# w_out kept in the second halves of w1 and w2, and a new list of the steps up to the first unit's outputs

## The chip, the cores and the metric

The kernel runs on one core of a Trainium2 chip. The core's engines run side by side, each in its own order: TensorE (PE, with its weight loads PEld), VectorE (DVE), ScalarE (ACT), GpSimd (POOL) and SyncE (SP, which here issues nearly all transfers). The metric is the device time of one execution in microseconds (us), and lower is better. Before the change the median of 5 runs is 592.6 us (591.66 to 593.51).

## The reference

Two blocks in a row, all in fp32 (q, k, v and beta arrive as fp32, the four moe weights as fp64). First a gated delta rule, token by token, for 4 batches of 8 heads, 768 tokens and 48 features:

```python
k_n = k / (norm(k) + 1e-6); state = 0
for t in range(768):
    y[t] = q[t] @ state
    state = state + beta[t] * outer(k_n[t], v[t] - state.T @ k_n[t])
```

Its outputs, as 3072 tokens of 384 features x, then go through a multiplicative feed-forward block:

```python
h = ((x @ w1) * (x @ w2)) @ w3        # w1, w2: 384 x 1024, w3: 1024 x 1024
out = h @ w_out                       # w_out: 1024 x 384
```

## The kernel before, in words

**Tiling.** The 768 tokens are cut into 12 chunks of 64. A chunk m of all 32 (batch, head) pairs is handled at once; two chunks make a unit u of 512 tokens for the feed-forward block. The delta rule of a chunk is solved by inverting a unit triangular matrix; the inverse is done for two chunks together, in blocks of 32, on DVE.

**w3 and w_out are folded** into one 1024 x 384 matrix w34 on the chip (line 756, `fold`), so that the block is ((x w1)*(x w2)) w34. The fold needs w3 transposed.

**The order is written out by hand.** Each kind of work is a Python generator, and every `yield` ends a step. `ORDER` is a list of names; each name runs its generator to its next yield, and the instructions of each engine stand in that order (the list is run from line 1006 on; `in_text_order` holds them to it). In this document V0.38 means the 38th entry of V0 in the list. The names, with m a chunk, j or u a unit:

- k, q, v: load a chunk's keys, queries, values. p: eight transfers each time, two times a chunk: keys, then queries, in the layout that DVE's transpose takes (`load_perm`, line 223). K, Q: transposes of the first two chunks on PE. d: those of the later chunks, on DVE.
- P0 to P35: a piece of weights (`piece`, line 695): transfer(s) into one of five buffers `raw`, two ACT instructions, two DVE instructions, one POOL instruction, which make fp32 of the bits of fp64. P0 to P7 are w_out, P8 to P23 w3 (one transfer each); P24 to P29 w1, P30 to P35 w2 (four transfers each). Of each weight, the first three pieces are columns 0 to 511, the next three columns 512 to 1023. A piece can be loaded when the piece five earlier has left its buffer.
- t0 to t15: transpose of a piece of w3. f0 to f7: a block of the fold, in two halves of eight matmul records on PE, then a copy by ACT.
- g: sums of squares of the keys of two chunks. N: their norms (15 small DVE instructions). s: the scores of a chunk (U on DVE, PT). u: U to DRAM (four transfers). V: the inverse of two chunks: V.2 loads Ub from DRAM, V.3 and V.4 copy to PSUM on ACT, then 31 steps of two DVE instructions (V0.5 to V0.35, lines 440 and 445), two ACT copies (V0.36, V0.37) and the store of Vd to DRAM (V0.38).
- e: the corner: eight transfers of the inverse out of DRAM (T), then two products on PE. n: scaled values on POOL. c: the chain of a chunk, which carries the state (line 551). y: its outputs (line 652), then ACT copies them into xT (y.2), and six transfers move rows inside xT (y.3).
- b0 to b7: the products with w1 and w2 of unit 0's first chunk; a00 to a07: those of its second chunk; a10 to a57: those of whole units (`ab`, line 772; three matmuls with w1, ACT copy, three with w2, DVE multiply). Block jc reads columns 128 jc to 128 jc + 127 of w1 and w2. T, S: sums of weights and of slabs for a Strassen product; o: that product (line 874); x: the results and their stores.

**Where w_out lies.** w1s and w2s are tiles of 128 x 3 x 1024. Until the folds are done, w_out (1024 x 384) lies in w2s and fills all of it, `wo = w2s[:]...rearrange("p (j d) -> p j d", d=DM)`. So P30 to P35 can write w2s only when the fold's matmuls that read that stretch are done. w1s is free from the start.

**Transfers.** SP's queue issues in the order of the list. The program as built gives its transfers eight semaphores in turn, so a transfer waits until the one eight before it has landed. ACT issues k0 and q0.

Of the kernel before, what the change touches and what calls it, by code (L numbers as in the profile page):

```python
# [8 lines left out]
FP32 = mybir.dt.float32  # L9
# [39 lines left out]
N1 P30 t12 t14 t15 e0 t15 d3 f7 d3 f6 e0 P30 P21 e0 e0 P24 f7 s2 s2 e1 e0 s2 P24 e0 e1 V1 p4 s2
e1 P26 s2 e1 P25 d3 c0 P21 P30 u2 s3 c0 s3 P26 N1 P31 P24 y0 s3 s3 y0 c0 s3 s3 P25 t13 N1 e1 u3  # L50
P31 c0 P26 P31 P32 c1 V1 c1 e1 P25 V1 P27 c1 V1 c1 V1 V1 t13 V1 V1 V1 V1 V1 V1 y0 V1 P25 f7 f6
f6 P30 P32 P32 v2 V1 P27 s1 P31 V1 V1 y1 b3 b1 V1 b0 P32 P28 y1 b1 V1 b1 b3 P29 P27 b2 b3 y1 V1
P27 b1 b0 P29 P29 c1 a01 b2 a03 P28 V1 a01 a00 b3 P28 P29 a02 a02 a03 P35 P28 V1 a05 b7 a00 V1
V1 V1 V1 a06 P33 V1 b5 a05 b7 b0 V1 P34 V1 b5 V1 a06 V1 V1 V1 P34 k4 V1 P35 V1 g2 a00 V1 k5 a00
b0 V1 V1 g2 a04 P34 n2 p4 n2 a07 c1 a04 b2 b4 P33 b6 b2 P35 V1 g2 g2 P34 g2 e2 a07 g2 P33 e2
P35 c2 c2 e3 d4 a03 d4 a03 a01 P33 g2 b4 d4 g2 e2 b6 e2 a07 e2 b4 d4 T a01 T b4 e2 a07 c2 s4 p5
g2 c2 T g2 N2 V2 b6 p5 b6 s4 b5 s4 c2 a06 c2 a06 a04 v3 y2 d5 b5 d5 k6 s4 e3 d5 s4 y2 a02 a05
d5 s4 b7 a04 n3 S0 a02 a05 S0 s5 S0 u4 e3 s5 n3 s5 e3 b7 T o0 c3 c3 s5 g3 s5 S0 N2 N2 x0 e3 g3
e3 o0 s5 c3 c3 u5 o0 x0 V2 S0 x0 y3 V2 y3 S0 V2 S0 V2 S0 S0 V2 V2 V2 S0 g3 o0 S0 o0 S0 x0 V2 c3
o0 v4 y3 V2 V2 V2 x0 p6 V2 x0 V2 S0 a10 a10 S0 g3 S0 x0 V2 x0 S0 o0 x0 x0 p6 a14 V2 k7 a17 a17  # L60
a14 V2 V2 V2 a15 a16 V2 a16 a15 V2 g3 V2 V2 V2 V2 V2 v5 V2 x0 a13 V2 V2 V2 a17 a12 V2 a13 g3 V2
V2 g3 a17 c3 a14 a13 d6 d6 a11 V2 e4 n4 a12 e4 e4 c4 d6 V3 e4 a14 a10 n4 g3 d6 c4 e5 a11 e4 s6
g3 a13 e4 a12 p7 a10 c4 g3 N3 s6 c4 s6 a11 y4 n5 y4 c4 e5 a12 c4 a11 a15 c5 n5 e5 p7 a16 d7 d7
d7 d7 o1 c5 v6 a16 k8 g4 g4 e5 g4 p8 a15 g4 s7 s7 S1 e5 s7 S1 e5 x1 s7 s7 S1 s7 c5 o1 s6 S1 u7
c5 o1 s6 s6 u6 S1 S1 V3 S1 y5 c5 c5 V3 V3 V3 V3 V3 o1 S1 x1 k9 S1 y5 S1 y5 o1 S1 S1 x1 x1 V3 S1
S1 V3 c6 V3 S1 S1 V3 d8 o1 x1 x1 v7 a20 n6 x1 V3 a20 o1 x1 a23 V3 V3 x1 V3 x1 n7 a27 a24 d8 a26
V3 V3 V3 V3 x1 g4 V3 a23 V3 a25 V3 a27 a27 V3 a24 V3 V3 a26 a20 V3 g4 V3 p8 V3 V3 V3 V3 p9 V3
V3 a25 d8 n6 d8 g4 a20 a22 a22 a24 V3 c6 a27 a25 a24 a21 a21 e6 e6 e6 g4 e7 N3 e6 a25 N3 g4 s8
g4 N4 s8 e6 a22 s8 a26 e6 c6 c6 N4 s8 a26 s8 y6 a22 V4 p9 N4 S2 d9 e7 s8 a21 e7 y6 u8 d9 a21 e7
c6 a23 d9 p10 e7 d9 S2 c6 S2 s9 n7 a23 s9 e7 o2 s9 c7 s9 S2 s9 k10 S2 c7 x2 o2 c7 S2 S2 o2 u9  # L70
s9 V4 c7 V4 S2 y7 V4 V4 x2 V4 g5 g5 V4 p10 d10 y7 S2 x2 S2 o2 y7 V4 o2 x2 c7 V4 V4 S2 S2 V4 o2
a35 x2 x2 k11 x2 S2 V4 x2 S2 a35 v8 V4 S2 V4 V4 S2 V4 x2 n8 o2 a37 x2 V4 v9 V4 V4 V4 x2 a34 n8
# [17 lines left out]
def kernel(  # L90
# [14 lines left out]
    P = 128  # L105
# [85 lines left out]
    TTs = padded("TT", [P, NR, H, C], 2)  # L191
# [340 lines left out]
    xts = {}  # L532

    def scaled_v(c):
        nv = vtoks[c]
        for r in range(NR):
            pool.tensor_tensor(  # L537
                out=nv[:, r], in0=nv[:, r],
                in1=scale_of(ns, c)[:, r].unsqueeze(2).to_broadcast([P, H, D]), op=ALU.mult,
            )  # L540
            yield

    def chain(c):
        TT, nv, KQ = TTs[c % 2], vtoks[c], KQs[c]

        def products(out, lhs, rhs):
            ps = two_banks()
# [23 lines left out]
            return St[feat(h % 2), z, NP * r + h // 2, :]  # L571

        St = Ss.get(c)
        R = nv
        if c > 0:
            ps = products(
                by_tokens_of_features, lambda r, h, z: KQ[feat(h % 2), NR * z + r, h // 2, 0, :], state
            )
            yield
            R = in_turn(work, [P, NR, H, D], "R", 1, "R")  # L580
            v3, r3 = (
                x[:].rearrange("p r (a e) d -> p (r a) e d", e=2) for x in (nv, R)
            )
            dve.tensor_tensor(
                out=r3, in0=v3, in1=ps.rearrange("p e g d -> p g e d"), op=ALU.subtract
            )
            yield
# [127 lines left out]
        pool.tensor_tensor(out=du, in0=du, in1=lo, op=ALU.add)  # L715
        yield

    w1s = const.tile([P, KM, DF], FP32, name="w1s")
    w2s = const.tile([P, KM, DF], FP32, name="w2s")
    w34 = const.tile([P, KF, DM], FP32, name="w34")  # L720

    wo = w2s[:].rearrange("p m f -> p (m f)").rearrange("p (j d) -> p j d", d=DM)

    def piece_wo(j):
        return piece(DM, [(slice(0, P), moe_w_out[j * P : (j + 1) * P, :])], lambda: wo[:, j])

    def piece_w12(w, src, m, n0):
        srcs = []
        for e in range(2):
            a, b = D * (NP * e + m), D * (NP * e + NP - 1) + 16 * m  # L730
            srcs.append((slice(C * e, C * e + D), src[a : a + D, n0 : n0 + CW]))
            srcs.append((slice(C * e + D, C * e + C), src[b : b + 16, n0 : n0 + CW]))
        return piece(CW, srcs, lambda: w[:, m, n0 : n0 + CW])

    w3s, w3Ts = {}, {}

# [19 lines left out]
    def fold(jc):  # L756
        ps = bank([P, CW])
        for kc in range(KF):
            pe.matmul(  # L759
                ps[:, 0:DM], lhsT=w3Ts[jc, kc // 4][:, kc % 4 * P : kc % 4 * P + P],  # L760
                rhs=wo[:, kc], start=(kc == 0), stop=(kc == KF - 1),
            )
            if kc == KF // 2 - 1:
                yield
        yield
        act.copy(out=w34[:, jc, :], in_=ps[:, 0:DM])
        yield
# [3 lines left out]

    def ab(u, jc, c0, c1):
        x = xts[u]
        js = slice(jc * P, (jc + 1) * P)

        def product(w):
            ps = bank([P, B, c1 - c0, C])
            for m in range(KM):
                pe.matmul(  # L779
                    ps[:].rearrange("p b c t -> p b (c t)"), lhsT=w[:, m, js],  # L780
                    rhs=x[:, m, :, c0:c1].rearrange("p b c t -> p b (c t)"),
                    start=(m == 0), stop=(m == KM - 1),
                )
            return ps[:].rearrange("p b c t -> p b (c t)")
# [260 lines left out]
```

## Time and profile before

| | |
|---|---|
| median of 5 runs | 592.6 us (591.66 to 593.51) |
| the profiled execution, device time | 595.21 us |
| its span, first to last instruction | 593.5 us |
| mean granted PE clock | 0.977 |
| PE busy | 544.5 us (92%) |
| DVE, ACT, POOL busy | 361.3, 159.5, 176.5 us |
| transfers | 57.31 MB, 219508 packets |

The profile shows one execution. A busy time is a sum over the instructions of an engine; a matmul's end is modelled, so a PE that is called busy is not at its peak. A fp32 matmul counts as two records on PE. "Idle before" is time of the engine just before an instruction, with what released it. The chain that ended last is followed back from the last instruction; its shares say which work stood on that chain, and 73% of it is PE, 10% DMA, 7% DVE, 4% SP's queue. PE's busy share in 40 equal slices begins 2, 5, 6 tenths and then stands at 8 or 9 nearly everywhere, and the granted clock drops to 7 or 8 tenths in slices 7 to 10.

### The profile page before, as it was taken

To read this page: it belongs to the slowest core of one execution; us is meant where nothing else is said; L and a number is where in the kernel's file an instruction comes from. 1 tells how busy PE (TensorE), PEld (TensorE's weight loads), DVE (VectorE), ACT (ScalarE), POOL (GpSimd) and SP (SyncE) were. 2 spreads that over 40 slices of the span, in tenths; PEclk is the share of its full clock that TensorE was granted. 3 is DMA by queue.
4 is the path that set the end of the run, shared out by engine and by line. 5 is a ranking of instruction groups with operands and counts; after the bars stand their busy time and mean duration, and the time that the engine had idled before them with its cause. 6 is when DMAs were issued, how large, how long until landed. Compare 5 with 4: busy or idle time off the path is not lost.

```text
span 593.5 us, 19063 instructions
## 1 busy us (share of the span) xinstructions
PE 544.5 (92%) x8188; PEld 381.1 (64%) x8188; DVE 361.3 (61%) x828; ACT 159.5 (27%) x333; POOL 176.5 (30%) x223
## 2 busy tenths in 40 slices
PE   2569889698999999999999989999999999999997
PEld 2456546576888974558854669645697446974477
DVE  3797896678786579574796555866736924210012
ACT  4666354452512202121210222112220112311100
POOL 7563542042364601206121043111170000600051
PEclk9999997778999999999999999999999999999999
DMA  9979986776855454563553345624432040010001
GB/s 248 201 158 271 204 166 139 130 168 136 144 83 94 99 85 109 80 97 51 116 98 80 48 66 102 127 56 62 71 54 88 13 90 4 17 41 13 1 0 53
DMA packets 219508, 57.31 MB, mean 97 GB/s; under 512 B 206657, under 2 KB 212801, under 8 KB 219425
## 3 DMA queue, kind: packets, MB, share of 16 engines
q1 hardware_dynamic: 215232, 55.31, 46.3%
q10 hardware_dynamic: 4192, 0.79, 1.0%
q8 instruction: 64, 1.05, 0.8%
q14 instruction: 20, 0.16, 0.1%
HBM read 43.88 MB, written 11.01 MB: 92 GB/s over the span
## 4 chain that ended last, share of the span: by engine, by line
PE 73%; DMA 10%; DVE 7%; SPq 4%; issue 3%; ACT 2%; POOL 0%; ACTq 0%; DVEq 0%; POOLq 0%
PE ps_f L779 42%; PE ps_f L874 17%; PE ps_w L551 5%; DMA raw<-in_moe_w_dram 4%; PE ps_w L652 4%; PE ps_w L498 2%; DMA Ub<-Ud 2%; PE ps_w L367 1%; DVE tb L440 1%; DVE ps_w L445 1%; DMA ktok<-in_k_dram 1%; PE ps_w L373 1%; SPq L414 1%; DMA vtok<-in_v_dram 1%; SPq L230 1%
## 5 line engine op out<-in xcount | busy, mean ns | idle before, releaser
L779 PE MATMUL ps_f<-xT,w2s 128*128 128x512 f32 (+1 forms) x336 | 131.8, 538 | 1.8 <-issue 1.8
L779 PE MATMUL ps_f<-xT,w1s 128*128 128x512 f32 (+1 forms) x336 | 129.8, 539 | 2.2 <-ACT raw L708 2.2
L846 POOL TENSOR_TENSOR ab<-ab 128x256 f32<-128x256 f32 x96 | 67.0, 726 | 177.4 <-DVE ab L795 155.3
L779 PEld LDWEIGHTS ps_f<-xT,w1s 128*128 128x128 f32 x336 | 64.5, 194 | 58.4 <-issue 52.7
L779 PEld LDWEIGHTS ps_f<-xT,w2s 128*128 128x128 f32 x336 | 62.1, 190 | 54.7 <-issue 51.6
L791 ACT COPY ab<-ps_f 128x512 f32<-128x512 f32 (+1 forms) x56 | 28.2, 526 | 170.3 <-PE ps_f L779 166.1
L874 PE MATMUL ps_f<-w,ab 128*128 128x192 f32 x376 | 66.5, 330 | 0.0
L795 DVE TENSOR_TENSOR ab<-ab,ps_f 128x512 f32<-128x512 f32 (+1 forms) x56 | 33.0, 603 | 52.8 <-PE ps_f L779 52.6
L874 PEld LDWEIGHTS ps_f<-w,ab 128*128 128x128 f32 x376 | 61.1, 190 | 4.4 <-issue 3.5
L440 DVE TENSOR_TENSOR tb<-Vb,Ub 128x31 f32<-128x31 f32 (+15 forms) x124 | 43.6, 352 | 19.4 <-DMA Ub<-Ud 16.1
L874 PE MATMUL ps_f<-room,ab 128*128 128x192 f32 x272 | 47.9, 330 | 1.9 <-DVE room L905 1.9
L445 DVE TENSOR_TENSOR Vb<-Vb,tb 128x31 f32<-128x31 f32 (+15 forms) x124 | 46.5, 375 | 4.3
L759 PE MATMUL ps_f<-w2s,w3T 128*128 128x384 f32 x128 | 46.2, 517 | 0.0
L874 PEld LDWEIGHTS ps_f<-room,ab 128*128 128x128 f32 x272 | 44.1, 190 | 2.8 <-issue 2.3
L673 ACT COPY xT<-ps_w 48x256 f32<-48x256 f32 x96 | 30.5, 365 | 55.8 <-PE ps_w L652 55.2
L270 POOL TENSOR_TENSOR sq<-ktok 128x384 f32<-128x384 f32 x24 | 20.9, 875 | 69.7 <-DMA ktok<-in_k_dram 62.3
L759 PEld LDWEIGHTS ps_f<-w2s,w3T 128*128 128x128 f32 x128 | 25.4, 204 | 16.8 <-issue 2.8
L537 POOL TENSOR_TENSOR vtok<-vtok,n 128x384 f32<-128x384 f32 x24 | 20.0, 845 | 43.2 <-DMA vtok<-in_v_dram 43.2
L367 PE MATMUL ps_w<-KQ 48*64 48x128 f32 x384 | 29.5, 293 | 1.7 <-DVE PT L397 1.7
L373 PE MATMUL ps_w<-KQ 48*64 48x64 f32 x768 | 29.9, 232 | 0.0
L715 POOL TENSOR_TENSOR w<-w,raw 128x512 uint32<-128x512 uint32 x16 | 20.9, 1310 | 27.7 <-ACT raw L708 4.4
L373 PEld LDWEIGHTS ps_w<-KQ 48*64 48x64 f32 x768 | 27.1, 146 | 0.1
(109 smaller groups left out, 659.0 us busy)
## 6 DMA issues: line engine op xcount, KB each, us to landing
raw<-in_moe_w_dram SPq DMA_DIRECT2D x16, 512.0 KB, 6.3
vtok<-in_v_dram SPq DMA_DIRECT2D x24, 192.0 KB, 4.3
raw<-in_moe_w_dram SPq DMA_DIRECT2D x24, 192.0 KB, 4.4
out_dram<-osb SPq DMA_DIRECT2D x46, 96.0 KB, 2.3
ktok<-in_k_dram SPq DMA_DIRECT2D x44, 96.0 KB, 3.8
raw<-in_moe_w_out_dram SPq DMA_DIRECT2D x8, 384.0 KB, 4.0
Ud<-U SPq DMA_DIRECT2D x48, 64.0 KB, 2.5
Ub<-Ud SPq DMA_DIRECT2D x6, 512.0 KB, 4.3
```

Source lines behind the costliest of these rows:

```text
L367: pe.matmul(ps[half(z), 0, n : n + 128], lhsT=x[:, 0, :], rhs=x.rearrange("p j t -> p (j t)"), start=True, stop=True,)
L373: pe.matmul(ps[half(z ^ j), 1, n + C * j : n + C * j + C], lhsT=x[:, 0, :], rhs=x[:, j, :], start=True, stop=True,)
L440: dve.tensor_tensor(out=tv, in0=V[:, 0 : s + 1, s : s + 1].to_broadcast([P, s + 1, n]), in1=U[:, s, s + 1 : BS].unsqueeze(1).to_broadcast( ...
L445: dve.tensor_tensor(out=o, in0=o, in1=tv, op=ALU.subtract)
L551: pe.matmul(out(ps, r, h, z), lhsT=lhs(r, h, z), rhs=rhs(r, h, z), start=True, stop=True,)
L673: act.copy(out=xT[f, p:NP:2, b : b + NR, cc, :].rearrange("p a r t -> p r a t"), in_=pyv[f, z, b : b + NR],)
L759: pe.matmul(ps[:, 0:DM], lhsT=w3Ts[jc, kc // 4][:, kc % 4 * P : kc % 4 * P + P], rhs=wo[:, kc], start=(kc == 0), stop=(kc == KF - 1),)
L779: pe.matmul(ps[:].rearrange("p b c t -> p b (c t)"), lhsT=w[:, m, js], rhs=x[:, m, :, c0:c1].rearrange("p b c t -> p b (c t)"), start=(m = ...
L791: act.copy(out=t, in_=ps)
L795: dve.tensor_tensor(out=t, in0=t, in1=ps, op=ALU.mult)
L846: pool.tensor_tensor(out=o_, in0=x_, in1=y_, op=op)
L874: pe.matmul(ps[b][:, b, :], lhsT=abs_[u, HF * f + i][:, t0 : t0 + P], rhs=ws_[w][:, i], start=first and i == 0 and (b == 0 or n == "F"), s ...
```

## The change

w_out now lies in the second halves of two tiles: w1s and w2s become 128 x 2 x 3 x 512 (half of the columns first), w_out's first four blocks lie in the second half of w1s and its last four in the second half of w2s. So the pieces of columns 0 to 511 (P24 to P26, P30 to P32) can be written at any time, and those of columns 512 to 1023 (P27 to P29, P33 to P35) only when the fold's matmuls that read there are done. The products `ab` address a half and a block in it.

The list's first 725 entries are permuted: the same names, each as often. The other 592 entries, from the first unit's outputs on, are unchanged. Two stretches of the list are shown, the beginning and that from the last steps of V0 to the first products of unit 0 (old first, then new). In `chain` and `scaled_v` the lookup of the values' tile is moved into the place of use, so that v may come later in the list.

```diff
 ORDER = """
-V0 P0 k0 beta P18 P13 P0 P18 P0 P0 P18 P18 g0 P11 beta P13 K0 K0 P11 P10 q0 P10 P3 k1 P11 P13
-K0 beta P12 g0 P3 K0 g0 K0 g0 P13 K1 g0 P8 P12 g0 K1 K1 P11 P9 Q0 Q0 g0 Q0 P10 P12 g0 Q0 Q0 g0
...
-P15 t6 P20 t7 V0 n1 P22 P20 V0 t7 d2 s0 V0 V0 f3 P23 P20 P22 t8 P21 V0 n0 P24 n0 f3 V0 V0 n1 t8
-V0 V0 t9 V0 V0 s2 p3 f4 f3 P23 P22 P26 g1 V0 g1 V0 f4 g1 P21 P22 P23 t14 d3 f4 P23 g1 t12 p3 V0
-N1 P30 t12 t14 t15 e0 t15 d3 f7 d3 f6 e0 P30 P21 e0 e0 P24 f7 s2 s2 e1 e0 s2 P24 e0 e1 V1 p4 s2
-e1 P26 s2 e1 P25 d3 c0 P21 P30 u2 s3 c0 s3 P26 N1 P31 P24 y0 s3 s3 y0 c0 s3 s3 P25 t13 N1 e1 u3
-P31 c0 P26 P31 P32 c1 V1 c1 e1 P25 V1 P27 c1 V1 c1 V1 V1 t13 V1 V1 V1 V1 V1 V1 y0 V1 P25 f7 f6
-f6 P30 P32 P32 v2 V1 P27 s1 P31 V1 V1 y1 b3 b1 V1 b0 P32 P28 y1 b1 V1 b1 b3 P29 P27 b2 b3 y1 V1
-P27 b1 b0 P29 P29 c1 a01 b2 a03 P28 V1 a01 a00 b3 P28 P29 a02 a02 a03 P35 P28 V1 a05 b7 a00 V1
-V1 V1 V1 a06 P33 V1 b5 a05 b7 b0 V1 P34 V1 b5 V1 a06 V1 V1 V1 P34 k4 V1 P35 V1 g2 a00 V1 k5 a00
-b0 V1 V1 g2 a04 P34 n2 p4 n2 a07 c1 a04 b2 b4 P33 b6 b2 P35 V1 g2 g2 P34 g2 e2 a07 g2 P33 e2
-P35 c2 c2 e3 d4 a03 d4 a03 a01 P33 g2 b4 d4 g2 e2 b6 e2 a07 e2 b4 d4 T a01 T b4 e2 a07 c2 s4 p5
...
+P12 k0 P0 K0 V0 P12 P12 P11 beta P0 P12 P8 P10 P11 P0 P8 P0 P1 P9 K0 g0 P8 P10 g0 g0 K0 P11 K0
+beta K0 q0 P9 k1 K1 P10 beta g0 P11 t4 P10 g0 K1 P2 K1 K1 q1 g0 P9 K1 g0 P8 g0 Q0 g0 t4 P9 g0
...
+t11 V0 t6 t8 f5 d2 n0 P21 P22 P24 t8 t6 P20 P20 f4 d2 f5 V0 V0 t9 t9 P21 s0 n1 f3 P23 t7 V0 f4
+p3 P23 V0 t7 P22 s1 V0 V0 n0 f4 s2 g1 P20 f3 V0 g1 V0 f3 P23 t12 g1 P22 g1 t15 t12 t15 P22 p3
+V0 P26 t14 d3 t14 f6 P24 g1 V1 N1 P24 P26 e0 e0 f7 e1 e0 s2 f7 s2 e0 e0 P30 e0 d3 s2 P30 P26 e1
+P21 s2 P21 s2 P26 p4 c0 c0 P24 d3 e1 d3 y0 t13 P25 e1 s3 s3 s3 y0 P31 s3 P25 c0 s3 s3 u2 P31 u3
+P32 t13 N1 e1 V1 e1 P29 c0 n1 c1 y0 P31 c1 V1 N1 P25 c1 V1 P32 P30 c1 P32 f7 P30 f6 P32 f6 y1
+P27 P29 P25 V1 V1 V1 b0 P28 b1 V1 V1 V1 V1 b0 V1 P31 V1 V1 V1 V1 P33 b0 b0 V1 y1 V1 V1 b2 V1 b1
+b1 c1 b2 y1 P27 P28 b2 b3 a00 b1 P29 a00 P33 a03 b3 v2 b2 P27 a02 P28 P34 P28 V1 a01 a02 V1 a01
+P27 P29 a00 V1 V1 V1 a03 V1 V1 a04 b7 V1 a00 V1 P34 V1 V1 k4 k5 V1 V1 b6 b7 V1 a04 b6 a01 V1
+a01 a06 V1 P34 g2 b3 g2 V1 g2 a06 P35 b3 b4 a05 b4 d4 a07 n2 P35 P35 P33 c1 p4 a05 V1 a03 n2
+P34 b5 e2 g2 P33 P35 a02 b5 c2 e2 a02 a07 e2 g2 g2 b5 c2 e2 g2 e2 a03 a05 g2 e3 a05 e2 d4 a06
...
@@ -532,16 +532,15 @@
     xts = {}
 
     def scaled_v(c):
-        nv = vtoks[c]
         for r in range(NR):
             pool.tensor_tensor(
-                out=nv[:, r], in0=nv[:, r],
+                out=vtoks[c][:, r], in0=vtoks[c][:, r],
                 in1=scale_of(ns, c)[:, r].unsqueeze(2).to_broadcast([P, H, D]), op=ALU.mult,
             )
             yield
 
     def chain(c):
-        TT, nv, KQ = TTs[c % 2], vtoks[c], KQs[c]
+        TT, KQ = TTs[c % 2], KQs[c]
 
         def products(out, lhs, rhs):
             ps = two_banks()
@@ -571,7 +570,7 @@
             return St[feat(h % 2), z, NP * r + h // 2, :]
 
         St = Ss.get(c)
-        R = nv
+        R = vtoks.get(c)
         if c > 0:
             ps = products(
                 by_tokens_of_features, lambda r, h, z: KQ[feat(h % 2), NR * z + r, h // 2, 0, :], state
@@ -579,7 +578,7 @@
             yield
             R = in_turn(work, [P, NR, H, D], "R", 1, "R")
             v3, r3 = (
-                x[:].rearrange("p r (a e) d -> p (r a) e d", e=2) for x in (nv, R)
+                x[:].rearrange("p r (a e) d -> p (r a) e d", e=2) for x in (vtoks[c], R)
             )
             dve.tensor_tensor(
                 out=r3, in0=v3, in1=ps.rearrange("p e g d -> p g e d"), op=ALU.subtract
@@ -715,14 +714,17 @@
         pool.tensor_tensor(out=du, in0=du, in1=lo, op=ALU.add)
         yield
 
-    w1s = const.tile([P, KM, DF], FP32, name="w1s")
-    w2s = const.tile([P, KM, DF], FP32, name="w2s")
+    w1s = const.tile([P, 2, KM, CW], FP32, name="w1s")
+    w2s = const.tile([P, 2, KM, CW], FP32, name="w2s")
     w34 = const.tile([P, KF, DM], FP32, name="w34")
 
-    wo = w2s[:].rearrange("p m f -> p (m f)").rearrange("p (j d) -> p j d", d=DM)
+
+    def wo(j):
+        x = (w1s, w2s)[2 * j // KF][:, 1].rearrange("p m f -> p (m f)")
+        return x[:, j % (KF // 2) * DM : j % (KF // 2) * DM + DM]
 
     def piece_wo(j):
-        return piece(DM, [(slice(0, P), moe_w_out[j * P : (j + 1) * P, :])], lambda: wo[:, j])
+        return piece(DM, [(slice(0, P), moe_w_out[j * P : (j + 1) * P, :])], lambda: wo(j))
 
     def piece_w12(w, src, m, n0):
         srcs = []
@@ -730,7 +732,7 @@
             a, b = D * (NP * e + m), D * (NP * e + NP - 1) + 16 * m
             srcs.append((slice(C * e, C * e + D), src[a : a + D, n0 : n0 + CW]))
             srcs.append((slice(C * e + D, C * e + C), src[b : b + 16, n0 : n0 + CW]))
-        return piece(CW, srcs, lambda: w[:, m, n0 : n0 + CW])
+        return piece(CW, srcs, lambda: w[:, n0 // CW, m])
 
     w3s, w3Ts = {}, {}
 
@@ -758,7 +760,7 @@
         for kc in range(KF):
             pe.matmul(
                 ps[:, 0:DM], lhsT=w3Ts[jc, kc // 4][:, kc % 4 * P : kc % 4 * P + P],
-                rhs=wo[:, kc], start=(kc == 0), stop=(kc == KF - 1),
+                rhs=wo(kc), start=(kc == 0), stop=(kc == KF - 1),
             )
             if kc == KF // 2 - 1:
                 yield
@@ -771,13 +773,14 @@
 
     def ab(u, jc, c0, c1):
         x = xts[u]
-        js = slice(jc * P, (jc + 1) * P)
+        hf, jx = divmod(jc, KF // 2)
+        js = slice(jx * P, (jx + 1) * P)
 
         def product(w):
             ps = bank([P, B, c1 - c0, C])
             for m in range(KM):
                 pe.matmul(
-                    ps[:].rearrange("p b c t -> p b (c t)"), lhsT=w[:, m, js],
+                    ps[:].rearrange("p b c t -> p b (c t)"), lhsT=w[:, hf, m, js],
                     rhs=x[:, m, :, c0:c1].rearrange("p b c t -> p b (c t)"),
                     start=(m == 0), stop=(m == KM - 1),
                 )
```

## Prediction

> **What bounds the kernel now.** I read the stages first, by cutting the profiled execution at events of the chain that ended last. The columns are the stretch in us, busy time and instructions of PE, PEld, DVE, ACT and POOL, the granted PE clock, the DMA share and GB/s:
>
> ```profile
> 0.00:51.30 51.30, 27.88 (x509) 23.67 (x510) 33.93 (x64) 30.64 (x56) 31.31 (x43) 0.97 0.93 213
> 51.30:84.10 32.80, 30.41 (x151) 18.48 (x149) 29.26 (x80) 14.80 (x27) 15.39 (x15) 1.00 0.91 211
> 84.10:104.50 20.40, 16.70 (x284) 10.56 (x283) 15.61 (x37) 10.23 (x18) 6.26 (x6) 0.83 0.72 137
> 104.50:141.50 37.00, 28.24 (x724) 23.79 (x724) 26.43 (x62) 18.42 (x42) 9.45 (x8) 0.82 0.67 138
> 141.50:146.30 4.80, 4.76 (x13) 3.48 (x14) 4.54 (x11) 0.41 (x2) 1.98 (x2) 0.64 0.70 179
> 146.30:270.00 123.70, 122.90 (x2097) 90.29 (x2099) 90.36 (x212) 29.20 (x67) 40.63 (x52) 1.00 0.59 100
> 270.00:593.50 323.50, 313.62 (x4420) 210.79 (x4420) 161.18 (x367) 55.82 (x124) 71.48 (x100) 1.00 0.29 57
> ```
>
> From 146.3 us to the end PE is busy 436.5 of 447.2 us at clock 1.00: it is the bound there, and the new list moves no step across its unchanged last 592 entries. Before 146.3 us PE is not the bound. So the end moves by what the start of PE's dense stretch moves, corrected by PE work done ahead of it. What sets that start is read from the chain that ended last (start, us, what):
>
> ```profile
> 45.78 5.46 DMA Ub<-Ud
> ...
> 88.41 3.84 DMA Vd<-Vb
> ...
> 104.47 0.91 PE ps_w L551 x38
> ...
> 141.55 21.72 PE ps_f L779 x90
> ```
>
> First the loads and scores until the inverse V0 gets its input (Ub); then V0 on DVE, 51.3 to 84.1 us, where DVE is busy 29.26 of 32.80 us; then V0's result through DRAM and into the corner e0; then chain c0 at 104.5; then a01, the first product with both chunks of tokens, at 141.5. Between these the SP queue, which issues the transfers in order, holds the chain:
>
> ```profile
> 73.64 8.57 SPq L230 DMA_DIRECT2D kperm<-in_k_dram  x8
> 82.31 1.82 SPq L699 DMA_DIRECT2D raw<-in_moe_w_dram  x4
> 84.23 4.08 SPq L230 DMA_DIRECT2D qperm<-in_q_dram  x8
> 88.41 0.43 SPq L453 DMA_DIRECT2D Vd<-Vb  x1
> ...
> 136.13 5.28 SPq L684 DMA_DIRECT2D xT<-xT  x6
> ```
>
> ACT ends V0.37 at 85.2 us, but Vd goes out at 88.4: p3, P26 and p3 stand ahead. The last row is y1.3, whose fourth transfer has landed at 141.4; a01's first matmul reads rows of the first and the fourth. PE waits for it, and then runs slowly:
>
> ```profile
> 138.39 0.94 PE L551 MATMUL ps_w<-X,ktok 64*48 64x48 f32 x64
> 141.54 12.66 PE L779 MATMUL ps_f<-xT,w1s 128*128 128x256 f32 x48 [2.21 <-ACT raw L708]
> ```
>
> The releaser named there, ACT's conversion of P28, belongs to columns that a01 does not read, so I take the transfer.
>
> **The change, part by part.** Instructions and transfers are the same in number and size; only addresses and order differ.
>
> *Place of w_out.* Before, w_out fills all of w2s, so P30 to P32 wait for the folds. ACT shows both waits: 5.56 us ahead of P30 at 96.65 us, and
>
> ```profile
> 127.82 0.48 ACT L766 COPY w<-ps_f 128x384 f32<-128x384 f32 x1 [5.30 <-PE ps_f L759]
> 128.20 0.67 ACT L707 ACTIVATE w2s<-raw 128x512 f32<-128x512 f32 x1
> ```
>
> the second for f6 ahead of P32. After, P24 to P26 and P30 to P32 go into free halves, and P27 to P29 and P33 to P35 wait for f6.2 instead. Nothing on the chain reads P30 to P32 before b1.3 at 134.4, so the two waits are worth nothing by themselves; what they allow is ACT's order. The new wait costs nothing either: in ACT's queue P29 stands directly behind f6.3, which waits for the same matmuls, and behind P29 stand b0.2 and y1.2. P29's two instructions take 0.66 us each, and y1.2 would be done about 130 us, ahead of its transfer's turn (below). Without that cover it would cost 1.3 us.
>
> *To V0's input.* Fifteen pieces of weights, k0 to k2, q0, q1 and one p stand ahead of Ub in both lists. k1 comes one piece later (pieces land 1.3 to 2.0 us apart at 11 to 16 us) and q0 about 4 us later on ACT, but ACT's 4.06 us wait for P12 at 22.1 is gone. Step by step from the rows: k1 landed about 20.5, K1 copied out 23.1, Q0 on PE to 25.6, the sums of squares across at 26, P1.3, then norms (3.7 us) to 31, P2.3 and four U products among DVE's other steps to 37.8, eight Ud transfers (5.9 us) to 43.7, landed 1.5 later: Ub issued at 45.4 against 45.8. Bounds 41 and 52. V0 then holds 32 us of DVE work against 31, so V0.37 is done at 85 to 86, about as before.
>
> *V0's way out.* P26's four issues (1.82 us) move behind Vd. Each transfer on this queue waits for the one eight before it, by the program's own semaphores, so p3's second part now waits for its first part alone (landed 82.3 to 84.6) and not for P26 (85.4 to 87.1): Vd goes out at 86.0, 2.4 us earlier. Bounds: 3.2 if SP is quite free, 0 if p3 takes as long as before. With its 3.84 us, e0's transfers start at 89.9 against 92.3.
>
> *To the a steps.* On SP from there to y1.3 stood 43.8 us. v2 (1.4) goes behind y1.3 and two pauses (1.9 and 0.9, a wait for U and one for a transfer) can close; P30 (2.1, ahead of e0 before) and P33 (2.0) come in. With pauses closed, 43.8 - 1.4 - 2.8 + 4.1 = 43.7; part of the transfers' waits on each other falls too (P28 and P29 took 3.1 and 2.6 us, against 1.8 for a like piece at 120.8), so I take 43.0, bounds 39 and 47. y1.3 starts at 132.9, its fourth transfer lands 5.3 us later, 138.2 against 141.4: **3.2 us**. y1 itself is not late: e1.3 stands behind c0.1 now, not ahead of it (it waited for T1 until 103.3), so c0.1 is at 101.0, and y1.1 at about 122.5 against 127.7.
>
> *Work done ahead.* Seven b products instead of six stand ahead of the first a on PE. Six matmul records of 256 columns take 1.3 us in the dense stretch: **1.3 us**.
>
> *The clock.* a01 and a03 took 2.2 and 2.5 us between starts against 1.3, at a granted clock of 0.64: 2.1 us lost. b0.1 waits for y0.3's fourth transfer, about 126.1; seven b's and c1.5 end at 136.2; PE waits 2.0 us for 138.2. That is like the 2.21 us before, so I count **0** of this; bounds 0 and 2.1.
>
> The Trainium skill, page "TensorE: Matmul & The Clock Gate", Part 1, says the clock is halved after an idle window of about 3.4 us. The row is harsher: 2.21 us without a matmul, behind thin ones, already came with 0.64. By the page the new wait would cost no clock and the sum would gain 2.1 us more; I go by the row.
>
> *Behind 146 us.* The steps up to o1 are also permuted (c4 ahead of most a1 steps), PE-bound before and after with DVE at 90 of 124 us. I count 0, bounds -3 (new stalls) and +1 (PE was idle 0.8 us).
>
> Sum: 3.2 + 1.3 + 0 = 4.5 us. The profiled span 593.5 becomes 589.0; with the 1.7 us around it, 595.2 becomes 590.7. The median of the runs shown is 592.6, 2.6 below the profiled execution, so the forecast for it is **588.1 us**.
>
> **Rivals.**
>
> *Saturated sooner.* If SP reaches y1.3 by 130 (the lower bound 39 us), the a's follow the b's without a pause, and y1.1's 5.2 us count in full, with the 2.2 us wait and the 2.1 of clock: 9.5 us, 583.1. For it: y1.1 has moved more than y1.3. Against: SP's rows sum to more.
>
> *Nothing moves.* If SP keeps its pauses and waits, 47 us from e0 to y1.3, the a's start at 142.2: 0.7 us later, paid by the seventh b, 592.0. It is also the case that w_out's place does nothing and the list only permutes work around the same SP queue.
>
> *Slower: the first loads.* DMA is at 0.93 in the first 51 us, so loads land in the order of issue. k2 is issued after P7, which waits on POOL for P8: about 24 against 21.3; its squares stand on DVE ahead of three of the U products. q1 took 8.0 us to land before. If q0 or k2 takes that long again behind a fuller queue, both norms and U slip 4 to 8 us and Ub is issued at 50 to 53. V0.37 passes SP's 86.0 for each us beyond 46, and all behind it shifts. It decides from Ub at 50.3 (4.5 us eaten); at 54 the time is 596. For it: seven pieces ahead of k1, not six. Against: ACT's 4 us at P12 is free.
>
> **How the numbers follow.** Forecast with its own range 585 to 591: 0.52. Saturated sooner, under 585: 0.20. Nothing moves: 0.10. Slower: 0.18. 0.2% of 592.6 is 1.2 us, about what a measurement can tell from no change. Faster 0.72, same 0.10, slower 0.18. The range 580.5 to 595 takes in the bounds on SP and half of the slow case, and leaves out about 0.05 below and 0.10 above.
>
> **What would show it.** In the profile after: Ub issued near 45; Vd out at 86, with only p3 ahead; no ACT wait ahead of P32; the xT transfers of y1 from 133; the first a near 138 with a PE wait of about 2 us before it and a clock under 1 behind it. I am wrong if Ub is issued after 48, if PE runs from y1 into the a's without a pause, or if a wait of more than 1 us on DVE or POOL opens between 146 and 270.

## The result, and the profile after

The changed kernel takes 596.84 us (median of 54 runs, 592.2 to 601.45), the kernel before 593.96 us (median of 94 runs, 589.96 to 601.87). The ratio is 1.0038, with a 95% interval of 1.0026 to 1.0051: about 2.3 us slower. (The ratio goes with the means, 596.3 to 594.1 us without the three slowest runs, which were disturbed; the medians lie further apart.) The forecast was 588.1 us, with a range of 580.5 to 595.

The profiled execution of the changed kernel is one of its shorter ones: 594.73 us, span 593.0, clock 0.971 (before: 595.21, 593.5, 0.977). The single traces differ by several us within one kernel, so two spans compared say nothing here. What can be compared are stretches, and waits that come back in every trace of one list.

The stages of the changed kernel, cut at the same times as before (stretch, busy time of PE, PEld, DVE, ACT, POOL, granted clock, DMA share, GB/s):

```profile
84.10:104.50 20.40, 18.73 (x426) 12.79 (x429) 17.59 (x45) 8.41 (x15) 6.26 (x7) 1.00 0.64 127
104.50:141.50 37.00, 28.12 (x647) 22.98 (x637) 22.98 (x55) 19.36 (x42) 7.07 (x6) 0.72 0.77 152
...
146.30:270.00 123.70, 121.46 (x2188) 88.74 (x2187) 96.21 (x216) 29.51 (x69) 44.13 (x55) 1.00 0.61 102
```

From 84 to 104 us PE was busy 2 us more than before, but in the next stretch the clock was 0.72 and not 0.82, and from 146 to 270 us PE was busy 121.46 us and not 122.90. The chain that ended last, between the first inverse and the products (start, us, what):

```profile
87.63 3.83 DMA Vd<-Vb
...
103.47 4.37 DMA raw<-in_moe_w_dram
...
129.03 2.19 DMA xT<-xT
...
131.35 8.61 PE ps_f L782 x30
```

Vd goes out 0.8 us sooner than before (88.41), not 2.4. Then P30's transfer stands on the chain, and at the end the rows of y0.3, not those of y1.3. SP's queue, in order of time (start, us, what), shows why:

```profile
87.63 0.43 SPq L453 DMA_DIRECT2D Vd<-Vb  x1
...
125.36 5.70 SPq L683 DMA_DIRECT2D xT<-xT  x6
131.15 5.63 SPq L698 DMA_DIRECT2D raw<-in_moe_w_dram  x12
137.47 4.64 SPq L683 DMA_DIRECT2D xT<-xT  x6
```

ACT in the same order, from P30's conversion on, with the idle time ahead of an instruction in brackets:

```profile
107.95 0.66 ACT L706 ACTIVATE w2s<-raw 128x512 f32<-128x512 f32 x1 [6.71 <-DMA raw<-in_moe_w_dram]
...
109.17 1.18 ACT L514 COPY T<-ps_w 32x512 f32<-32x512 f32 x2
```

From Vd to y0.3 SP issues 58 transfers in 37.7 us; before, 54 in 34.3 us (88.41 to 122.70). That is 0.64 to 0.65 us each in both, so the four more (P26's) are 2.6 of the 3.4 us (an estimate from these rows). So y0.3 is at 125.4 and y1.3 at 137.5 (before: 122.7 and 136.1). On ACT, P30's conversion waits 6.71 us for its transfer, with e1.4 and y0.2 behind it. PE then waits for y0.3 ahead of the first b (its row):

```profile
131.35 4.63 PE L782 MATMUL ps_f<-xT,w1s 128*128 128x256 f32 x12 [1.58 <-DMA xT<-xT]
```

Later PE stops once more:

```profile
176.53 0.66 PE L651 MATMUL ps_w<-KQ,S 48*48 48x64 f32 x32
177.01 0.89 PE L550 MATMUL ps_w<-X,ktok 64*48 64x48 f32 x61
179.33 0.29 PE L550 MATMUL ps_w<-X,ktok 64*48 64x48 f32 x3 [1.43 <-issue]
179.55 4.15 PE L782 MATMUL ps_f<-xT,w2s 128*128 128x256 f32 x18
```

These rows are y2.1's end and c2.5, 64 records of one product. After 61 of them PE stands 1.43 us, and the profile names no releaser ("issue"). The old list has no stop there.

### The profile page after: what moved, and what is told of

Its sections match the earlier page's. It is cut to its first block, busy times and chain, and to the rows that moved or that the text cites. A ratio compares the mean times of both kernels' runs of the same rounds, so it can differ in the third digit from the quotient of the medians.

```text
span 593.0 us, 19060 instructions
## 1 busy us (share of the span) xinstructions
PE 543.4 (92%) x8188; PEld 379.4 (64%) x8188; DVE 365.0 (62%) x828; ACT 159.8 (27%) x333; POOL 176.6 (30%) x223
## 4 chain that ended last, share of the span: by engine, by line
PE 75%; DMA 8%; DVE 6%; SPq 4%; issue 3%; ACT 3%; ACTq 0%; POOL 0%; DVEq 0%; POOLq 0%
PE ps_f L782 43%; PE ps_f L877 17%; PE ps_w L550 5%; PE ps_w L651 3%; PE ps_w L498 2%; DMA Ub<-Ud 2%; DMA ktok<-in_k_dram 2%; PE ps_w L367 2%; SPq L230 1%; PE ps_w L373 1%; DMA raw<-in_moe_w_dram 1%; DMA X<-in_q_dram 1%; DVE tb L440 1%; SPq L462 1%; ACT KQ L347 1%
## 5 line engine op out<-in xcount | busy, mean ns | idle before, releaser
L440 DVE TENSOR_TENSOR tb<-Vb,Ub 128x31 f32<-128x31 f32 (+15 forms) x124 | 45.5, 367 | 16.8 <-DMA Ub<-Ud 13.3
L445 DVE TENSOR_TENSOR Vb<-Vb,tb 128x31 f32<-128x31 f32 (+15 forms) x124 | 45.2, 364 | 4.3
L379 DVE TENSOR_TENSOR U<-ps_w,wt 128x512 f32<-128x512 f32 x24 | 16.4, 687 | 26.9 <-PE ps_w L373 26.1
L367 PEld LDWEIGHTS ps_w<-KQ 48*64 48x64 f32 x384 | 23.3, 144 | 12.6 <-ACT T L514 4.6
L373 PEld LDWEIGHTS ps_w<-KQ 48*64 48x64 f32 x768 | 26.9, 146 | 0.0
```

What stands on the lines that cost most here:

```text
L367: pe.matmul(ps[half(z), 0, n : n + 128], lhsT=x[:, 0, :], rhs=x.rearrange("p j t -> p (j t)"), start=True, stop=True,)
L373: pe.matmul(ps[half(z ^ j), 1, n + C * j : n + C * j + C], lhsT=x[:, 0, :], rhs=x[:, j, :], start=True, stop=True,)
L440: dve.tensor_tensor(out=tv, in0=V[:, 0 : s + 1, s : s + 1].to_broadcast([P, s + 1, n]), in1=U[:, s, s + 1 : BS].unsqueeze(1).to_broadcast( ...
L445: dve.tensor_tensor(out=o, in0=o, in1=tv, op=ALU.subtract)
```

## The experiments

A ratio is to the kernel before, measured beside it on the same chip, with its 95% interval. Moves are written with entry numbers: c2.5 is the fifth c2 of the list. A line of a diff shows a few entries in their order, and other entries can stand between them. The kernels start from the changed one unless the text says otherwise.

**place_only** and **list_only** take the two parts of the change alone. The first is the changed kernel with the old list (its diff begins as below), the second the old kernel with the new list:

```diff
-P12 k0 P0 K0 V0 P12 P12 P11 beta P0
+V0 P0 k0 beta P18 P13 P0 P18 P0 P0
...
```

> The list of before, with w_out in the second halves of w1 and w2. Theory A (the new list lost the time, above all by ACT's wait for P30's transfer, 101.2 to 107.95 us in the profile after, with e1.4 and y0.2 behind it): the place alone is worth 0, 593 to 595 us, ACT's 5.3 us wait ahead of P32 is gone and P27 takes a wait for f6.2 in its stead. Theory B (the place costs: new waits of P27 to P29 and P33 to P35 for f6.2): 1 to 3 us slower than before.

> The new list, with w_out in w2 as before. Theory A: as the changed kernel within 1 us (ratio 1.002 to 1.005), since P30 waits for its transfer and not for the fold, and only P32 waits 1 to 2 us for f6.2. Theory B: as before (ratio 1.000). If the new place is what lets the new list run, 2 us slower than the changed kernel.

place_only: 592.88 us against 592.39, ratio 1.0010 (0.9986 to 1.0034). No cost or gain of the place by itself is seen. list_only: 596.95 us, 1.0069 (1.0044 to 1.0094, 6 runs), nearest to the third case forecast, 2 us slower than the changed kernel. Without the place, P32's conversion stands ahead of f6.2 in the list and writes into w_out's last blocks, so the fold reads overwritten values, and PE waits 2.6 us for P32 ahead of f6.2. So the place is what lets this list compute the right thing, and the list is where the time is. Theory B fell.

**p30_late** takes P30's conversion on ACT out of the way of e1.4 and y0.2:

```diff
-e0.6 P30.2 e1.4 y0.2 P25.2
+e0.6 e1.4 y0.2 P30.2 P25.2
```

> The changed kernel with one step moved: P30's two ACT instructions behind y0.2 and not ahead of e1.4. Theory A: e1.4 starts near 104 and not at 109.2, s3, c0.3 and c1.1 follow 3 to 5 us sooner, U is stored sooner and y1.3 with it; 2 to 4 us faster than the changed kernel, ratio to before 0.997 to 1.001. Theory C (the loss stands in the first loads: Ub landed at 53.3 and not at 51.2): the same as the changed kernel, ratio 1.004, since SP's queue to y1.3 has no room. Theory D (the loss stands behind 146 us, where DVE is busy 96 us and not 90): the same as the changed kernel too.

595.19 us, 1.0043 (1.0021 to 1.0065): nothing won, so theory A fell. ACT's rows show where the gain went:

```profile
104.59 1.18 ACT L514 COPY T<-ps_w 32x512 f32<-32x512 f32 x2 [2.91 <-PE ps_w L498]
...
108.40 0.68 ACT L706 ACTIVATE w2s<-raw 128x512 f32<-128x512 f32 x1
...
118.00 0.67 ACT L706 ACTIVATE w1s<-raw 128x512 f32<-128x512 f32 x1 [8.33 <-DMA raw<-in_moe_w_dram]
```

e1.4 is at 104.6 and not 109.2, and c1.1 starts at 113.7 and not 118.4, as forecast. But ACT then waits 8.33 us for P25's transfer with e1.6 behind it, and c1.3 is at 122.6, 1.0 us later than in the changed kernel. The wait moved to the next transfer that SP issues late.

**early_after** has the new list to V0.2 and then what is left in the old order.

```diff
-V0.2 k3.1 V0.3 d2.2 P4.3 P18.2 g1.4 f0.1 t2.2
+V0.2 P18.2 P18.3 P18.4 t2.2 s1.7 t10.1 P14.1 g1.4
...
```

> The changed kernel's list up to the load of Ub (V0.2), then what is left in the order of before; w_out in its new place. Theory C (the first loads cost the 2 us): Ub lands near 53 us, the inverse and all behind it 2 us later, ratio to before 1.003 to 1.005. Theories A and D: the early part costs nothing that lasts, ratio 0.999 to 1.001.

599.52 us, 1.0127 (1.0104 to 1.0150, 6 runs), more than any theory gave. It settles nothing: Ub goes out at 46.8 as in the new list, but what is left of the old order does not fit the pieces already loaded, DVE waits 9.0 us for ACT's conversions between 45 and 95 us, and V0.37 ends at 93.2 and not 87.1.

**thin_apart** moves one step, c2.5, behind the next big product:

```diff
-y2.1 c2.5 a04.3
+y2.1 a04.3 c2.5
```

> The changed kernel with the last products of c2 (c2.5, 64 matmul records) behind a04.3 and not directly behind y2.1 (128 records). In three traces of the new list PE stops inside c2.5, at its record 2245, for 1.4 to 1.9 us with no releaser, and the two traces of the old list have no such stop there. Theory E (some 250 short records in a row outrun what feeds PE's queue): the stop is gone or under 0.5 us, 1 to 2 us faster than the changed kernel, ratio to before 1.000 to 1.003. Theory F (the stop is a wait for c2.5's operands or banks): it stays, ratio 1.004.

593.77 us against 593.94, 1.0006 (0.9975 to 1.0037). The same place in its trace:

```profile
178.23 0.67 PE L651 MATMUL ps_w<-KQ,S 48*48 48x64 f32 x32
178.82 1.56 PE L782 MATMUL ps_f<-xT,w2s 128*128 128x256 f32 x6
180.32 0.84 PE L550 MATMUL ps_w<-X,ktok 64*48 64x48 f32 x55
181.45 0.33 PE L550 MATMUL ps_w<-X,ktok 64*48 64x48 f32 x9 [0.30 <-issue]
```

The stop is down from 1.43 to 0.30 us, and the time is that of the kernel before. That is theory E's forecast, not theory F's.

**y_first** brings the first outputs forward on ACT and SP:

```diff
-V1.2 P29.1 y0.3 P27.1 P28.1 P33.1 y1.3 v2.1
+V1.2 y0.3 P29.1 P27.1 P28.1 y1.3 P33.1 v2.1
-f6.3 y1.1 P29.2 b0.2 y1.2 b1.2 b2.2 P27.2
+f6.3 y1.1 y1.2 b0.2 b1.2 b2.2 P29.2 P27.2
-a00.2 P33.2 b3.2 a02.2        P28.4 P27.4 P29.4
+a00.2 b3.2 a02.2 P33.2        P29.4 P27.4 P28.4
```

> The changed kernel with the first outputs ahead on ACT and SP: y1.2 directly behind y1.1, P29's transfers and conversion behind y0.3 and y1.2, P33's behind y1.3. Theory G (SP's queue, at 0.65 to 0.68 us for each transfer, sets the start of PE's dense stretch; the new list has 57 transfers from Vd to y0.3 where the old one has 53): y0.3 starts near 123 and not at 125.4, b0.1 near 130 and not at 131.4, y1.3 near 135 and not at 137.5; 1.5 to 3 us faster than the changed kernel, ratio to before 0.999 to 1.002. Theory E alone (the loss is the stop in c2.5): the a's and b's start sooner but the time is that of the changed kernel within 1 us.

596.70 us, 1.0052 (1.0019 to 1.0084). All that was forecast of the places came: y0.3 at 122.3 (125.4), b0.1 at 129.9 (131.4) with no wait, the first a at 140.1 (143.5). The time did not follow. PE gives part of it back (its rows; DVE's product of a00 frees a bank late, and the clock falls behind the stop):

```profile
146.61 4.18 PE L782 MATMUL ps_f<-xT,w1s 128*128 128x256 f32 x18
152.82 2.03 PE L782 MATMUL ps_f<-xT,w2s 128*128 128x256 f32 x6 [2.03 <-DVE ab L798]
```

**y_first_thin** has y_first's edits and thin_apart's:

```diff
-y2.1 c2.5 a04.3
+y2.1 a04.3 c2.5
```

> Both edits of the two kernels before this. Theories E and G together: their gains add, 2.5 to 5 us faster than the changed kernel, ratio to before 0.996 to 1.000. If one of them is wrong: no better than the other alone.

593.94 us against 593.94, 1.0010 (0.9984 to 1.0036). The step c2.5 is worth 2.8 us in the medians; y_first's edits add nothing to it.

**k0_first** puts the first loads about as before:

```diff
-P12.1 k0.1 P0.1 K0.1 V0.1 P12.2 P12.3 P11.1 beta.1 P0.2
+k0.1 P0.1 K0.1 V0.1 beta.1 P12.1 P11.1 P0.2 P0.3 P12.2 P12.3
```

> The changed kernel with the first loads in about the order of before: P0, k0 and beta ahead of P12 and P11. Theory C (the loss comes from the first loads: k0's last part lands at 12.0 and not at 9.1 us, Ub at 53.3 and not at 51.2): k0 lands near 9, Ub 1 to 2 us sooner, and 1 to 2 us faster than the changed kernel, ratio 1.000 to 1.002. Theory G: the inverse ends 1 to 2 us sooner but Vd still goes out near 87.5 behind p3, so within 0.5 us of the changed kernel, ratio 1.003 to 1.005.

594.69 us, 1.0023 (0.9995 to 1.0051). Ub went out at 46.2 (47.5) and Vd at 86.3 (87.6), so Vd followed, against theory G's number. A gain of 1 us is possible, but the intervals of the two kernels overlap, and in k0_thin (below), with the same first loads, Ub went out at 47.7 and Vd at 89.7: not settled. In this trace the stop was 1.89 us, and the clock behind it was halved:

```profile
178.00:180.00 2.00, 0.50 (x4) 0.45 (x5) 1.54 (x8) 1.52 (x5) 0.00 (x0) 0.99 0.54 74
180.00:182.00 2.00, 2.00 (x6) 1.54 (x6) 1.96 (x3) 0.00 (x0) 0.00 (x0) 0.50 0.70 94
```

**k0_thin** is k0_first with thin_apart's move, a third pair with and without the stop:

```diff
-y2.1 c2.5 a04.3
+y2.1 a04.3 c2.5
```

> The changed kernel with k0_first's order of the first loads and thin_apart's place of c2.5: a third pair with and without the stop in c2.5. Theory E (the stop costs 1.3 to 1.9 us and now and then 1.4 to 1.8 us of clock behind it): 1.5 to 3 us faster than k0_first, ratio to before 0.997 to 1.001. If the two earlier pairs were chance: the time of k0_first, ratio 1.001 to 1.004.

592.31 us against 593.15, 0.9986 (0.9961 to 1.0011), as theory E said, and c2.5 runs without a stop:

```profile
179.47 0.94 PE L550 MATMUL ps_w<-X,ktok 64*48 64x48 f32 x64
```

It has the lowest ratio of the complete kernels, and the measurement can't tell it from the kernel before.

**thin_joined** makes the same neighbourhood in the old kernel:

```diff
-c2.5 a06.3 c2.6 a06.4 a04.3 v3.1 y2.1
+y2.1 c2.5 a06.3 c2.6 a06.4 a04.3 v3.1
```

> The kernel before with one step moved: y2.1 (128 short matmul records) directly ahead of c2.5 (64 records), as in the new list; all else, w_out's place too, is of before. Theory E (short records in a row outrun the feed of PE's instructions): a stop without releaser of 1.3 to 1.9 us inside c2.5, which ends 1.2 to 1.6 us after an instruction packet, in some runs with the clock at 0.5 for 3.4 us behind it; 1.5 to 3 us slower than before, ratio 1.002 to 1.005. Theory H (the two thin_apart kernels were faster by another effect of the moved step): no stop, ratio 0.999 to 1.001.

594.97 us against 594.12, 1.0014 (0.9990 to 1.0038): a miss of theory E. PE waits 0.5 us for DVE ahead of c2.5 and stops only 0.3 us inside it, not 1.3 to 1.9. Short records side by side are not enough; see the next section.

**u_first** and **u_first2** try to start the second inverse sooner, on top of k0_first, y_first and thin_apart:

```diff
-p4.1 P25.1 P31.1 u2.1 u3.1 P32.1 V1.2
+p4.1 u2.1 u3.1 V1.2 P25.1 P31.1 P32.1
-P30.2 e1.4 y0.2 P25.2 P31.2 t13.2 e1.6 V1.3 V1.4
+e1.4 y0.2 P30.2 t13.2 e1.6 V1.3 V1.4 P25.2 P31.2
-P31.3 c1.2 P25.3 P30.3 c1.4        V1.28 a00.4
+c1.2 c1.4 P30.3 P25.3 V1.7 P31.3   V1.24 a00.4
```

> The changed kernel with all the edits so far (k0, y and thin) and with the second inverse's way ahead: on SP the two stores of U and the load of Ub (V1.2) ahead of P25, P31 and P32; on ACT P30, P25 and P31 converted behind y0.2 and V1.4; on DVE c1.2 and c1.4 ahead of the conversions, and a00.4 earlier. Theory J (after y_first the bound from 130 to 166 us is DVE's second inverse, which ended at 157.5 whatever SP did, and it starts when SP gets to U and Ub): Ub lands near 121 and not at 127 to 129, the inverse ends near 153, c2.1 runs near 160 and not 164 to 166; 3 to 5 us faster than y_first_thin, ratio to before 0.992 to 0.997. If DVE is not the bound there: the time of y_first_thin, ratio 0.999 to 1.002. If b0.1 waits for P25 and b0.3 for P31, now later on SP: ratio above 1.000.

> As u_first, but nothing of the first outputs stands behind a transfer of P31 or P32: on ACT f7.3, f6.3 and y1.2 ahead of P31's and P32's conversions, on DVE P25's, P31's and P32's conversions inside the second inverse, on PE b0.1, b1.1, b2.1 ahead of b0.3. In u_first b0.1 waited 5.6 us for f6.3, which stood behind P32's landing on ACT. Theory J (DVE's second inverse bounds the stretch to 166 us): b0.1 near 130, the inverse ends at 153 to 155 and not 157.5 to 160.6, c2.1 near 161 to 163; 2 to 4 us faster than y_first_thin, ratio to before 0.994 to 0.998. If DVE is not the bound: the time of y_first_thin, ratio 0.999 to 1.002.

u_first: 595.96 us, 1.0019 (0.9990 to 1.0048). Ub's load was issued at 116.8 and not 122, but f6.3 now stood on ACT behind P32's landing, and b0.1 waited 5.6 us for its bank. u_first2 put these in order:

```diff
-P25.2 P31.2 P32.2 f7.3 f6.3 y1.2     b0.1 b1.1 b0.3 b2.1
+P25.2 f7.3 f6.3 y1.2 P31.2 P32.2     b0.1 b1.1 b2.1 b0.3
```

It took 598.14 us, 1.0068 (1.0030 to 1.0106). V1.5 began at 121.3 and not 127 to 129, but V1.37 still ended at 159.3. Neither kernel tells what bounds this stretch: they made waits of their own.

**half_thin** and **half_yf** are thin_apart and y_first_thin with DVE relieved: 15 of the 31 subtractions of the second inverse are left out.

```diff
-            dve.tensor_tensor(out=o, in0=o, in1=tv, op=ALU.subtract)
+            if j != 1 or s % 2 == 0:
+                dve.tensor_tensor(out=o, in0=o, in1=tv, op=ALU.subtract)
```

> thin_apart with 15 of the 31 subtractions of the second inverse (V1) left out, so the inverse of chunks 2 and 3 is not complete: about 5.5 us less DVE work between 129 and 158 us. Theory J (DVE's second inverse is where early starts of PE are given back): V1.37 ends near 152 and not at 158.5, but PE's dense stretch still starts at 132 behind y0.3, so little is won: 0 to 1.5 us faster than thin_apart, ratio to before 0.998 to 1.001. If DVE's chain alone sets the end: 4 to 5 us faster, ratio 0.992.

> y_first_thin with the same 15 subtractions left out (the inverse of chunks 2 and 3 is not complete). Theory J: the stops of PE at a01.3 and e2.3 (1.9 and 1.2 us in y_first_thin) go, and the 3 us by which the first products start sooner stay: 2 to 4 us faster than half_thin and than y_first_thin, ratio to before 0.993 to 0.997. If the gain of y_first is lost elsewhere (clock, SP, PE's feed): as half_thin, ratio 0.998 to 1.001.

half_thin: 593.75 us, 1.0014 (0.9984 to 1.0043). half_yf: 595.01 us, 1.0017 (0.9989 to 1.0045). No gain is seen, so DVE alone is not it, and theory J's gain of 2 to 4 us did not come. In half_yf V1.37 ended at 152.3, but the store of its result stayed where it was, as SP's queue shows:

```profile
153.05 5.43 SPq L230 DMA_DIRECT2D qperm<-in_q_dram  x8
158.58 0.43 SPq L454 DMA_DIRECT2D Vd<-Vb  x1
162.17 1.90 SPq L463 DMA_DIRECT2D TT<-Vd  x4
```

PE's rows, c2.1 and e2.3, have the wait that follows:

```profile
162.20 1.15 PE L551 MATMUL ps_w<-S,KQ 48*64 48x48 f32 x64
166.43 1.13 PE L499 MATMUL ps_w<-T,U 33*33 33x32 f32 x64 [3.09 <-DVE T L482]
```

**half_vd** moves that one transfer:

```diff
-p4.2 V1.38
+V1.38 p4.2
```

> half_yf (15 of the 31 subtractions of the second inverse left out) with its result's store to DRAM (V1.38) ahead of p4's eight transfers on SP. In half_yf V1.37 ended at 152.3, 5.2 us sooner than in y_first_thin, but the store went out at 158.6 as before, behind p4, and PE stopped 3.3 us for e2.3 at 166.4. Theory K (SP's queue takes back what DVE or the first products win): the store goes out near 153, e2's transfers near 158.7 and not 162.2, e2.3 follows c2.1 at 163 with no stop over 0.5 us, and the time is 2 to 4 us below half_yf's, ratio to before 0.994 to 0.999. If the stop is not SP's, or what follows takes the gain back again: ratio 1.000 to 1.003.

591.90 us against 592.75, 0.9986 (0.9957 to 1.0015): 0.0031 or 1.8 us below half_yf, with intervals that overlap. SP's queue:

```profile
153.71 0.37 SPq L454 DMA_DIRECT2D Vd<-Vb  x1
154.12 5.93 SPq L230 DMA_DIRECT2D qperm<-in_q_dram  x8
160.10 2.08 SPq L463 DMA_DIRECT2D TT<-Vd  x4
```

And PE at the same two steps:

```profile
162.77 1.15 PE L551 MATMUL ps_w<-S,KQ 48*64 48x48 f32 x64
164.35 0.75 PE L499 MATMUL ps_w<-T,U 33*33 33x32 f32 x64 [0.43 <-DVE T L482]
```

e2's transfers start at 160.1 (forecast 158.7), and PE's stop is 0.43 us and not 3.09. So with DVE relieved it is SP's turn for one store that decides here whether PE stops; the time follows by about the size of the stop, as far as the intervals allow to say. In the complete kernel y_first_thin both have to come together: there V1.37 ends at 157.5 and the store goes out at 158.6, so this move alone could win 1 us at most, and it was not tried.

## Why the prediction was wrong

**The loss is the stop in c2.5.** The step of the prediction that failed here is "Behind 146 us ... I count 0". Its bounds (-3 for new stalls) would have held the loss, but the only stalls named as signs were waits on DVE and POOL; what came is a wait of PE for its own instructions. Three pairs of kernels differ only by the place of c2.5: 1.0038 and 1.0006, 1.0052 and 1.0010, 1.0023 and 0.9986. Each pair's intervals overlap, but the three differences are 0.0032, 0.0042 and 0.0037, on average 0.0037 or 2.2 us, which is all of the 2.3 us that the change lost. (Worked out from the six intervals, the average is good to about 0.0022, so it is clear of zero.) The traces give the same size: in the five traces with the two steps joined in the new list the stop is 1.31 to 1.91 us (mean 1.6), and in two of the five the clock is 0.5 for 3.4 us behind it, which costs the next products 1.7 us (18 records in 5.84 and 5.83 us, 4.15 in the changed kernel). 1.6 + 2/5 x 1.7 = 2.3.

What PE waits for is read from the packets of the "instruction" kind that the trace records, 16384 bytes each. There are 64 of them (queue q8 of the page), and PE runs 16376 matmuls and weight loads and 168 other instructions, some 258 for each packet. Around the stops without releaser (us):

```
kernel                       PE stops          packet            PE goes on after its end by
changed, c2.5                177.91 to 179.33  176.67 to 177.94  1.39
p30_late, c2.5               179.44 to 181.34  178.88 to 179.76  1.58
list_only, c2.5              179.78 to 181.35  179.16 to 180.12  1.23
y_first, c2.5                178.70 to 180.02  177.84 to 178.80  1.22
k0_first, c2.5               177.61 to 179.50  177.15 to 178.08  1.42
before, record 5038          344.33 to 346.12  343.38 to 344.82  1.30
```

In all five c2.5 stops PE halts at the same record, 2245, and goes on 1.2 to 1.6 us after the packet's last byte. No row names a releaser, so that PE waits for the packet is inferred, but the traces leave little room for another reading.

Number all of PE's matmuls, weight loads and other instructions in order of start. The stop in c2.5 then stands at number 4545 in all five traces. Over all 17 traces, 62 of the 64 stops of more than 0.25 us without releaser stand 193 or 194 beyond a multiple of 256, whatever work is there. So a packet holds 256 instructions, and these are its borders. With border and packet paired in order, PE went on at least 1.20 us after the packet's end at every one of 63 borders in each trace, and the packet began when PE was 7 to 301 instructions short of the border. In the changed kernel PE ran 166 instructions between the start of c2.5's packet and the stop. c2.5's 64 records and their weight loads are 128 instructions in under 1 us; six records of a big product are 12 in 1.3 us. So a packet that is asked for late in y2.1 comes too late when c2.5 follows, and in time when a04.3 does. thin_joined fits this: its border is number 4545 too, again inside c2.5, but the packet came 0.6 us sooner than in the changed kernel (176.08 to 177.00, y2.1 from 174.9 in both) and c2.5 was held 0.5 us by DVE, so PE had little left to wait for and went on 1.34 us after the packet's end. What sets when a packet starts was not tried. The old list has such stops too (2.27 us at 108.9 us, 1.79 at 344.3), but not here.

The Trainium skill, page "Runtime: NRT & Kernel Launch", section "Instruction fetch mechanics", says that the stream comes in blocks of 256 instructions and that fetching is hidden, because dispatch is slower than the fill. The 16384-byte packets and the borders 256 apart agree; "hidden" does not hold here, where PE stopped 1.3 to 1.9 us. Page "TensorE: Matmul & The Clock Gate", Part 1, ties the halved clock to an idle window of about 3.4 us. The length agrees (the half clock lasts 3.4 us), but in c2.5 stops of 1.89 and 1.91 us were enough for it, while those of 1.31 to 1.57 us were not. The length of a stop alone does not decide: near record 5037 a stop of 1.93 us has the half clock behind it in k0_thin and u_first2, and none in the changed kernel, y_first, y_first_thin and half_thin.

**The gain did not come, because SP's queue was mis-sized.** The sum was 3.2 + 1.3 + 0. Its first term rested on "43.0, bounds 39 and 47" from e0 to y1.3; measured were 45.9 us in the changed kernel (91.5 to 137.5), so y1.3 starts 1.3 us later than before and the term of 3.2 us is a small loss. The two pauses are gone as gaps between rows of SP, but their time is not: the eight stores of U took 7.05 us, 2.87 and 1.96 before, and a transfer from Vd to y0.3 still took 0.65 us on average. "Vd out at 86.0" was 87.6, since p3 was reached 3.8 us later (77.5, before 73.6). The steps one by one:

- Ub issued near 45.4: 47.5 in the changed kernel, 46.2 to 48.1 in the other traces with its first loads; landed 53.3 (before 51.2). Inside the bounds, 2 us late. k0's last part lands at 12.0 and not 9.1, behind P12; the rival on the first loads had the mechanism, but not the size.
- c0.1 near 101.0: 101.3, right.
- y1.1 near 122.5: 127.4. The prediction took away the waits of ACT for the folds and did not ask what P30 and P25 wait for in their new places: their own transfers, 6.7 and 3.2 us. p30_late shows that this by itself is worth nothing, since c1.3 waits for the next one.
- Seven b's ahead of the first a: right. But PE's pause did not stay ahead of the a's; it moved to b0.1, 1.58 us for y0.3, which I had seen at "about 126.1" and which landed at 131.2.
- "The clock: 0" held in sum: before, half clock from 142.8 to 146.2; after, from 132.6 to 136.0.
- The place is worth nothing by itself: right (1.0010, interval across 1).

The rival "Nothing moves", at 47 us from e0 to y1.3, came nearest for this part.

**The ground of the sum failed too.** "So the end moves by what the start of PE's dense stretch moves" does not hold in these kernels. With no stop of over 0.3 us in c2.5 in either, the first a is at 144.2 us in thin_apart and at 140.0 in y_first_thin, and the times are the same (1.0006, 1.0010). So even with SP free the 3.2 us would have been worth little. In y_first_thin's trace PE stops 1.76 us for DVE at 150.5 and 0.98 us at e2.3, at 165.3, with half the clock from 167.3 to 170.8. half_yf and half_vd suggest that SP's next turn, the store of the second inverse, is behind the stop at e2.3, but their times overlap; in y_first_thin the inverse's end and that store lie within 1.1 us of each other.

**What stays open.** Whether the order of the first loads is worth its 1 us; what takes back an earlier start of the a's in a complete kernel; and whether a complete kernel can keep y_first's start by moving the second inverse and its store forward together. u_first and u_first2 did not manage it.

## What to carry to other kernels

Where a list orders many short steps, count each queue's transfers between two points of the chain and multiply by that queue's measured pitch: here 0.65 us on SP gave the lateness that a reading of pauses missed. Before a conversion or copy is moved ahead, ask when its own transfer lands, not only what it waited for in its old place. And count PE's instructions as well as its time: a stretch of short matmuls can starve PE, and here a big product between two short stretches won 2.2 us, where the reorderings of the waits that were tried won nothing that could be measured.

## What the runs showed that I had not expected

- PE's instruction stream comes in 16384-byte packets, and PE waits for it, at borders 256 instructions apart: 1.3 to 1.9 us at one place of the new list, and 0.8 to 2.0 us near record 5037 in every trace of both lists, among short records.
- A stop of 1.9 us without matmuls can have half the granted clock behind it for 3.4 us, in the middle of PE's dense stretch (p30_late, k0_first), at a further cost of 1.7 us; elsewhere a stop of 1.93 us had none.
- A first a that comes 4.2 us sooner can leave the time unchanged (y_first_thin beside thin_apart). That one store's turn on SP (158.6 us in y_first_thin and in half_yf) sets a later meeting point is likely, not shown.
